# Linear-attention state added by one product of 384 columns instead of two of 192, with the step order laid out anew

## The chip, the cores and the metric

The kernel runs on one core of one Trainium2 chip. The metric is the device time of one execution in microseconds (us). It is launched several times; medians are given with the number of runs. The profile is one separate execution, so its span (start of the first to end of the last instruction) is not quite the time of a timed run. Where two kernels were timed in the same rounds on the same chip, the ratio is the mean of one kernel's fast runs over the mean of the other's fast runs of the same rounds. It is therefore not quite the ratio of the medians. A run counts as slow when it is over 1.5% above the fastest of its kernel.

TensorE is written PE in the profile, its weight loads PEld, VectorE DVE, ScalarE ACT, GpSimd POOL, SyncE SP. SP issues the loads.

## The reference

Two blocks follow one another. The first is a recurrent attention with a decay per step and channel, over 4 batches of 8 heads, 768 steps and 48 channels:

```
for t in range(S):
    cur = einsum('bhd,bhe->bhde', u * k[t], v[t])
    y[t] = einsum('bhd,bhde->bhe', r[t], state + cur)
    state = w[t][..., None] * state + einsum('bhd,bhe->bhde', k[t], v[t])
```

The second mixes the tokens of one batch (x is y with the heads side by side, 768 x 384):

```
W_tok = scale * (x @ w_q) @ (x @ w_k).T
out   = relu(W_tok @ x) @ w_out
```

## The kernel before

It works in 12 units of 256 steps, three per batch. A unit goes through some 30 steps on five engines: the log of w, running sums of it by matmul, exponentials, decayed r and k, transposes, the score matrix and its mask, the new state, the output. All matmuls go through one helper, so in the profile nearly all of TensorE has one line. Its groups are told apart by their tiles: cw are the running sums of the log (step `sums`), psT the transposes of decayed k and r (KdS, RdS), A the scores and AmB the masked ones, Sn the new state and SB the carried one, Y the output (`ymat` from the masked scores, `yst` from SB, `yd` from Vd), xt_ps, qk, Tps, mps and fps the products of the second block (fps is `fin`). A shape such as 64\*128 is the part of the array that a product uses, rows by columns. The parts that matter here:

```python
def load(n, nm, ap):                       # w, k, r, v of unit n, 384 KB each, from SyncE
    ...
    t = ld.tile([C, H, D2], F32, name=nm + "G", tag=nm + "G")     # 3 buffers each
    nc.sync.dma_start(out=t, in_=src.rearrange("h (p j) d -> p h (j d)", j=2))

def kdec(n):                               # GpSimd: decayed k, "Kd"
    nc.gpsimd.tensor_tensor(pad(T["Kd", n]), jhd(T["k", n]), hd(T["em", n]), ALU.mult)

def stadd(n, q):                           # adds the carried state to the new one, in PSUM
    if 2 * m + q:
        SB = T["SB", b, 2 * m + q]
        for hh in range(2):                # two products, each on 64 columns of the array
            mm(T["Sn", n][ds(hh * 64, 64), q, 0:DM].rearrange(...)[:, :, hh],
               ID128[:, ds(hh * 64, 64)],
               SB.rearrange(...)[:, :, hh], start=False)

def yst(n):                                # output from the state: full array
    ... mm(T["Y", n][:, q, ...], T["RKT", n][:, 0, q, hp], SB[:, ...], start=False)

def yd(n):                                 # output from u*k*r*v: 64 rows at a time
    ... mm(T["Y", n][:, q, 0:DM], PERM[ds(q * HC, HC), j], T["Vd", n][ds(q * HC, HC), j]...)
```

The order on every engine is fixed by a table. Each step has a time in the table (the unit's start plus an offset), all steps are sorted by it, and every engine executes its instructions in that order. The loads have a table of their own; only its order counts, together with the three buffers of each input:

```python
    steps = [ (-3.67, log, ()), (-1.33, uk1, ()), (-0.45, sums, ()), ...
              (15.25, ymat, ()), (15.48, yst, ()), (15.48, yd, ()), ... ]
    start  = [0.42, 8.84, 16.14, 23.73, 31.34, 38.86, ...]
    lstart = [-100, -99, -98, -11.4, -9.09, 4.54, 0.63, 6.68, 49.1, 51.23, 17.9, 58.9]
    ...
    for _, _, fn in sorted(plan, key=lambda x: x[:2]):
        fn()
```

## Time and profile before

| | kernel before |
|---|---|
| time, median of 3 runs | 123.15 us (122.78 to 123.25) |
| profiled span | 122.0 us, mean granted clock 0.971 |

Three lines of the page of the kernel before carry what the prediction only tells. The first is the busy time of each engine, its share of the span and its instructions. The second is the clock that TensorE was granted, in tenths of full speed, for 40 equal slices of the span. The third is the chain that ended last, by engine.
```profile
PE 100.1 (82%) x1822; PEld 64.6 (53%) x1822; DVE 91.8 (75%) x150; ACT 77.2 (63%) x146; POOL 84.7 (69%) x81
...
PEclk9999996799999999999999999999999999999985
...
PE 68%; ACT 12%; DVE 6%; DMA 3%; POOL 3%; issue 2%; ACTq 1%; SPq 1%; DVEq 0%
```
TensorE sets the pace of the middle of the kernel. By the page its clock falls once before the last slices, in the two slices from 18 to 24 us. The first products were slow too, though the page shows no lower clock there: two of 384 columns stood 0.33 us apart at 12.96 us, against 0.17 at 42.91.

### The profile page before, as it was taken

What the parts mean: (1) busy time and instruction counts of PE and PEld (TensorE: products, weight loads), DVE (VectorE), ACT (ScalarE), POOL (GpSimd) and SP (SyncE); (2) the same over time, 40 slices, a digit from 0 to 9 for tenths busy, and PEclk for the clock granted to TensorE, in tenths of its full rate; (3) what the DMA queues carried; (4) which work ended last, traced back from release to release, by engine and by line L of the source; (5) the groups of instructions that cost most, each with busy time, mean ns of one, the idle gap of its engine ahead of it and who ended that gap; (6) DMA issues with size and microseconds to landing.
All of it is one profiled execution on the core that took longest, in us unless ns stands there. A gap on an engine that the chain in (4) does not pass through costs nothing.

```text
span 122.0 us, 4284 instructions
## 1 busy us (share of the span) xinstructions
PE 100.1 (82%) x1822; PEld 64.6 (53%) x1822; DVE 91.8 (75%) x150; ACT 77.2 (63%) x146; POOL 84.7 (69%) x81
## 2 busy tenths in 40 slices
PE   0193938979898999999999899999999999966800
PEld 0133536557575766757657466576576666532400
DVE  6213596699798978999989998989989777253800
ACT  4236391689779868986685948976478966426000
POOL 8949899995999999599597995967839804000000
PEclk9999996799999999999999999999999999999985
DMA  3999999999999999899839999500552200573092
GB/s 77 322 325 325 323 320 341 292 232 318 236 256 273 288 300 263 230 266 247 245 75 329 348 269 252 149 0 0 134 129 52 82 5 0 129 181 85 24 283 83
DMA packets 54598, 24.66 MB, mean 202 GB/s; under 512 B 51121, under 2 KB 54578, under 8 KB 54578
## 3 DMA queue, kind: packets, MB, share of 16 engines
q1 hardware_dynamic: 52274, 21.24, 64.6%
q10 hardware_dynamic: 2304, 3.15, 9.1%
q8 instruction: 14, 0.23, 0.7%
q14 instruction: 6, 0.05, 0.1%
HBM read 19.66 MB, written 4.72 MB: 200 GB/s over the span
## 4 chain that ended last, share of the span: by engine, by line
PE 68%; ACT 12%; DVE 6%; DMA 3%; POOL 3%; issue 2%; ACTq 1%; SPq 1%; DVEq 0%
PE cw L66 12%; PE Y L66 11%; PE psT L66 10%; PE fps L66 10%; PE Sn L66 5%; PE A L66 5%; PE xt_ps L66 5%; PE qk L66 5%; PE Tps L66 4%; ACT X L130 3%; DMA u<-in_u_dram 3%; DVE AmB L244 3%; ACT XT L130 2%; PE mps L66 2%; POOL uk L250 1%
## 5 line engine op out<-in xcount | busy, mean ns | idle before, releaser
L244 DVE TENSOR_TENSOR AmB<-A,MASK 128x1024 bf16<-128x1024 f32 x24 | 28.8, 1219 | 1.3 <-PE A L66 1.2
L271 POOL TENSOR_TENSOR Vd<-V,diag 128x768 bf16<-128x768 bf16 x12 | 17.7, 1478 | 13.7 <-ACT X L130 3.4
L250 POOL TENSOR_TENSOR uk<-kG,ubc 128x768 f32<-128x768 f32 x12 | 21.8, 1816 | 1.7 <-DVE ubc L486 1.7
L178 ACT ACTIVATE em<-cw,bias 128x384 bf16<-128x384 f32 x24 | 13.0, 580 | 15.6 <-PE cw L66 15.6
L257 POOL TENSOR_TENSOR uk<-uk,rG 128x768 f32<-128x768 f32 x12 | 21.8, 1816 | 0.1
L207 POOL TENSOR_TENSOR KdS<-kG,em 128x768 bf16<-128x768 f32 x12 | 19.7, 1640 | 1.2 <-ACT em L178 1.2
L227 DVE COPY RKT<-psT 128x2048 bf16<-128x2048 bf16 x12 | 14.6, 1217 | 4.0 <-PE psT L66 4.0
L66 PEld LDWEIGHTS <-KdS 64*128 64x128 bf16 (+1 forms) x256 | 10.8, 99 | 9.1 <-POOL KdS L207 3.6
L200 DVE TENSOR_TENSOR RdS<-rG,cw 128x384 bf16<-128x384 f32 x24 | 12.2, 551 | 4.5 <-ACT cw L185 4.5
L66 PE MATMUL fps<-wout_sb,mixT 128*128 128x384 bf16 x72 | 14.6, 328 | 0.1
L302 DVE TENSOR_TENSOR SB<-Sn,pt 128x384 bf16<-128x384 f32 x20 | 11.0, 551 | 4.0 <-PE Sn L66 2.6
L66 PEld LDWEIGHTS <-RKT 48*64 48x64 bf16 (+1 forms) x464 | 10.3, 107 | 7.1 <-issue 4.5
L185 ACT ACTIVATE cw<-cw,bias 128x384 f32<-128x384 f32 x24 | 12.3, 553 | 0.2
L264 DVE TENSOR_REDUCE diag<-uk 128x16 f32<-128x768 f32 x12 | 11.3, 945 | 0.4 <-POOL uk L257 0.4
L155 ACT ACTIVATE logw<-wG 128x768 bf16<-128x768 f32 x12 | 10.2, 851 | 2.1 <-DMA wG<-in_w_dram 2.1
L66 PE MATMUL cw<-logw,BI 128*128 128x384 bf16 x36 | 11.5, 377 | 0.0
L66 PE MATMUL psT<-ID,KdS 128*128 128x128 bf16 x96 | 7.8, 227 | 4.0 <-DVE AmB L244 2.0
L66 PE MATMUL cw<-logw,BS 128*128 128x384 bf16 x36 | 11.0, 363 | 0.0
L66 PE MATMUL A<-RKT 48*64 48x128 bf16 x384 | 10.1, 226 | 0.8 <-ACT X L130 0.8
L130 ACT CAST X<-Y 128x768 bf16<-128x768 f32 x11 | 8.8, 800 | 2.9 <-PE Y L66 2.7
L211 ACT CAST V<-vG 128x768 bf16<-128x768 f32 x12 | 10.0, 841 | 0.0
L130 ACT COPY osb<-fps 128x384 f32<-128x384 f32 x13 | 6.1, 484 | 5.3 <-PE fps L66 2.1
(74 smaller groups left out, 165.1 us busy)
## 6 DMA issues: line engine op xcount, KB each, us to landing
wG<-in_w_dram SPq DMA_DIRECT2D x12, 384.0 KB, 5.5
kG<-in_k_dram SPq DMA_DIRECT2D x12, 384.0 KB, 5.1
rG<-in_r_dram SPq DMA_DIRECT2D x12, 384.0 KB, 4.8
vG<-in_v_dram SPq DMA_DIRECT2D x12, 384.0 KB, 4.9
out_dram<-osb ACTq DMA_DIRECT2D x16, 192.0 KB, 3.0
out_dram<-osb SPq DMA_DIRECT2D x8, 192.0 KB, 3.8
wout_f<-in_moe_w_out_dram SPq DMA_DIRECT2D x1, 576.0 KB, 4.7
wq_f<-in_moe_w_q_dram SPq DMA_DIRECT2D x1, 96.0 KB, 4.1
```

Source lines behind the costliest of these rows:

```text
L66: nc.tensor.matmul(o, l, rr, start=start, stop=stop, skip_group_check=True, is_transpose=trans)
L130: (nc.scalar.copy if e else nc.vector.tensor_copy)(o, i)
L178: nc.scalar.activation(em[:, j], T["cw", n, 1 + j][:, 0:DM], ACT.Exp, bias=bias[2 + j], scale=-1.0)
L185: nc.scalar.activation(cw, cw, ACT.Exp, bias=bias[j], scale=1.0)
L200: nc.vector.tensor_tensor(pad(Rd)[:, j], jhd(T["r", n])[:, j], T["cw", n, j][:, 0:DM].rearrange("p (h d) -> p h d", d=D), ALU.mult)
L207: nc.gpsimd.tensor_tensor(pad(T["Kd", n]), jhd(T["k", n]), hd(T["em", n]), ALU.mult)
L227: nc.vector.tensor_copy(RKT, T["psT", n])
L244: nc.vector.tensor_tensor(T["AmB", n][:, js].rearrange("p q h t -> p h q t"), T["A", n, js], _rep(_rep(MASK[:, js], 1, NP), 1, 2), ALU.mult)
L250: nc.gpsimd.tensor_tensor(uk, T["k", n].rearrange("p h (j d) -> p h j d", j=2), _rep(ubc.rearrange("p (h d) -> p h d", d=D), 2, 2), ALU.mult)
L257: nc.gpsimd.tensor_tensor(uk, uk, T["r", n].rearrange("p h (j d) -> p h j d", j=2), ALU.mult)
L264: nc.vector.tensor_reduce(diag.rearrange("p j h -> p h j"), T["uk", n], axis=AX.X, op=ALU.add)
L271: nc.gpsimd.tensor_tensor(Vd, T["V2", n], _rep(T["diag", n], 3, D), ALU.mult)
```

## The change

The intent: the two half-array products of `stadd` become one product over the whole array, which has the same shape as its usual neighbours, and the whole table of times is laid out anew around it.

```diff
-            for hh in range(2):
-                mm(T["Sn", n][ds(hh * 64, 64), q, 0:DM].rearrange(
-                    "p (q h d) -> p q h d", h=2, d=D)[:, :, hh],
-                   ID128[:, ds(hh * 64, 64)],
-                   SB.rearrange("p (q h d) -> p q h d", h=2, d=D)[:, :, hh], start=False)
+            mm(T["Sn", n][:, q, 0:DM], ID128, SB, start=False)
```

The new tables, cut to the rows that the argument uses:

```diff
     steps = [
-        (-3.67, log, ()),
-        (-1.33, uk1, ()),
-        (-0.45, sums, ()),
+        (-4.17, log, ()),
+        (-2.11, uk1, ()),
+        (-1.82, uk2, ()),
+        (-1.25, sums, ()),
         ...
-        (3.56, uk2, ()),
         ...
-        (15.25, ymat, ()),
-        (15.48, yst, ()),
-        (15.48, yd, ()),
+        (14.85, ymat, ()),
+        (14.88, yd, ()),
+        (15.08, yst, ()),
...
-    start = [0.42, 8.84, 16.14, 23.73, 31.34, 38.86, ...]
+    start = [0.58, 8.99, 16.15, 23.89, 31.49, 39.01, ...]
-    lstart = [-100, -99, -98, -11.4, -9.09, 4.54, 0.63, 6.68, 49.1, 51.23, 17.9, 58.9]
+    lstart = [-100, -99, -98, -17.38, -15.07, -5.06, -7.06, -6.47, 43.12, 46.19, 13.3, 52.91]
```

Cut away: the other rows of `steps`, the tables of the first and last unit and of the second block, four small tables that say whether ScalarE or VectorE makes a copy and which queue stores an output, the places of the weights' load and cast, a new layout of XT with the same element counts, and a transpose by DMA that stays switched off.

More of the change, by code (lines that the diff above doesn't have):

```diff
@@ L45 @@
     EX = (1, 1, 1, 1, 1, 1, 1, 1, 1, 1, 1, 0)
-    ET = (1, 1, 1, 1, 0, 0, 0, 0, 0, 1, 1, 0)
+    ET = (0, 1, 1, 1, 0, 0, 0, 0, 1, 1, 1, 0)
     EQ = (1, 0, 1, 0, 0, 0, 1, 0, 1, 1, 1, 0)
-    EM = (1, 1, 1, 0, 1, 0, 0, 1, 1, 0, 1, 1, 1, 1, 1, 1, 1, 1, 1, 0, 1, 1, 0, 1)
-    EF = (0, 1, 0, 1, 1, 1, 1, 0, 0, 1, 1, 0, 1, 1, 1, 1, 1, 1, 0, 0, 0, 0, 0, 0)
-    ES = (1, 0, 0, 1, 0, 1, 1, 1, 1, 1, 1, 0, 1, 1, 1, 1, 1, 1, 0, 1, 0, 1, 0, 0)
+    EM = (1, 1, 1, 0, 1, 0, 1, 0, 1, 0, 1, 1, 1, 1, 0, 1, 1, 1, 1, 0, 1, 1, 0, 1)
+    EF = (0, 1, 0, 1, 1, 1, 1, 0, 0, 1, 1, 0, 1, 1, 1, 1, 1, 1, 1, 1, 0, 0, 0, 0)
+    DT = (0, 0, 0, 0, 0, 0, 0, 0, 0, 0, 0, 0)
+    ES = (1, 0, 0, 1, 0, 1, 0, 1, 1, 1, 1, 0, 1, 1, 1, 0, 1, 0, 0, 1, 0, 1, 0, 0)
     NCH = S // C
@@ L343, in yev @@
             T["X", b] = xpool.tile([C, NCH, DM], BF16, name="X", tag="X")
-            T["XT", b] = xpool.tile([128, NK, S], BF16, name="XT", tag="XT")
+            T["XT", b] = xpool.tile([128, NCH, NK, C], BF16, name="XT", tag="XT")
             T["qk", b] = xpool.tile([128, NU, 4, DH], BF16, name="qks", tag="qks")
@@ L350, in xtr @@
         b, m = divmod(n, NU)
-        tp = mtile([128, NK, C2], BF16, "xt_ps")
+        if DT[n]:
+            nc.sync.dma_start_transpose(
+                out=T["XT", b][:, ds(2 * m, 2)].rearrange("p c k t -> p (c k) t"),
+                in_=T["X", b][:, ds(2 * m, 2)].rearrange("p c d -> p (c d)"))
+            return
+        tp = mtile([128, 2, NK, C], BF16, "xt_ps")
         for cc in range(2):
             for dt in range(NK):
-                mm(tp[:, dt, ds(cc * C, C)],
+                mm(tp[:, cc, dt],
                    T["X", b][:, 2 * m + cc, ds(dt * 128, 128)], ID128, trans=True)
@@ L360, in xev @@
         b, m = divmod(n, NU)
-        copy(ET[n], T["XT", b][:, :, ds(m * C2, C2)], T["tp", n])
+        if not DT[n]:
+            copy(ET[n], T["XT", b][:, ds(2 * m, 2)], T["tp", n])
     def qkmat(n):
@@ L371, in qkmat @@
             for kt in range(NK):
-                mm(qk[:, cc], XT[:, kt, ds((2 * m + cc) * C, C)], wk_sb[:, kt],
+                mm(qk[:, cc], XT[:, 2 * m + cc, kt], wk_sb[:, kt],
                    start=(cc == 0 and kt == 0))
@@ L376, in qkmat @@
                 mm(qk[ds(q * DH, DH), 2:4].rearrange("p c h -> p (c h)"), T["wq"][:, kt],
-                   XT[:, kt, ds((2 * m + q) * C, C)], start=False)
+                   XT[:, 2 * m + q, kt], start=False)
         T["qkp", n] = qk
@@ L501 @@
     steps = [
-        (-3.67, log, ()),
-        (-1.33, uk1, ()),
-        (-0.45, sums, ()),
-        (-0.42, expk, ()),
-        (-0.25, expr, ()),
-        (1.36, kdec, ()),
-        (1.89, rdec, ()),
-        (2.24, decay, ()),
-        (3.56, uk2, ()),
-        (5.7, trR, (1, )),
-        (5.95, trR, (0, )),
-        (5.99, vcast, ()),
-        (6.48, red, ()),
-        (6.51, vd, ()),
-        (7.46, evT, ()),
-        (8.59, amat, (0, )),
-        (9.91, amat, (1, )),
-        (10.1, mask, (0, )),
@@ L520 @@
-        (10.73, mask, (1, )),
-        (11.87, state, ()),
-        (11.9, stadd, (0, )),
-        (12.36, stev, (0, )),
-        (13.55, stadd, (1, )),
-        (14.38, stev, (1, )),
-        (15.25, ymat, ()),
-        (15.48, yst, ()),
-        (15.48, yd, ()),
-        (15.51, yev, ()),
-        (17.44, xtr, ()),
-        (18.18, xev, ()),
-        (20.45, qkmat, ()),
-        (20.75, qkev, ()),
+        (-4.17, log, ()),
+        (-2.11, uk1, ()),
+        (-1.82, uk2, ()),
+        (-1.25, sums, ()),
@@ new lines @@
+        (-0.85, expk, ()),
+        (-0.85, expr, ()),
+        (1.26, rdec, ()),
+        (1.84, decay, ()),
+        (2.32, kdec, ()),
+        (4.44, red, ()),
+        (5.37, trR, (1, )),
+        (5.66, trR, (0, )),
+        (6.06, vcast, ()),
+        (6.09, vd, ()),
+        (7.05, evT, ()),
+        (8.19, amat, (0, )),
+        (9.36, mask, (0, )),
+        (9.6, amat, (1, )),
+        (10.86, mask, (1, )),
+        (11.18, state, ()),
+        (11.21, stadd, (0, )),
+        (11.65, stev, (0, )),
@@ L534 @@
+        (13.15, stadd, (1, )),
+        (14.23, stev, (1, )),
+        (14.85, ymat, ()),
+        (14.88, yd, ()),
+        (15.08, yst, ()),
+        (15.11, yev, ()),
+        (16.78, xtr, ()),
+        (17.5, xev, ()),
+        (20.15, qkmat, ()),
+        (20.18, qkev, ()),
     ]
     first = [
-        (-6.23, log, ()),
-        (-6.05, sums, ()),
-        (-2.68, expk, ()),
-        (-0.31, decay, ()),
-        (0.59, uk1, ()),
-        (1.7, expr, ()),
-        (3.15, kdec, ()),
-        (5.93, trR, (1, )),
@@ L544 @@
-        (6.95, rdec, ()),
-        (6.98, trR, (0, )),
-        (7.64, evT, ()),
-        (8.73, uk2, ()),
-        (9.1, red, ()),
-        (9.65, amat, (0, )),
-        (9.93, amat, (1, )),
-        (11.0, mask, (0, )),
-        (12.22, mask, (1, )),
-        (13.97, vcast, ()),
-        (14.21, state, ()),
-        (14.64, stadd, (0, )),
-        (15.85, ymat, ()),
-        (16.28, stev, (0, )),
-        (16.31, stadd, (1, )),
-        (16.31, yst, ()),
-        (16.86, stev, (1, )),
-        (16.87, vd, ()),
@@ L562 @@
-        (16.9, yd, ()),
-        (17.07, yev, ()),
-        (18.09, xtr, ()),
-        (18.76, xev, ()),
-        (20.43, qkmat, ()),
-        (20.46, qkev, ()),
+        (-6.35, log, ()),
+        (-6.32, sums, ()),
+        (-6.09, uk1, ()),
+        (-3.08, expk, ()),
+        (-0.77, decay, ()),
+        (-0.04, expr, ()),
+        (2.81, kdec, ()),
+        (2.84, trR, (1, )),
+        (6.35, rdec, ()),
+        (6.57, trR, (0, )),
+        (7.24, evT, ()),
+        (8.41, uk2, ()),
+        (8.44, amat, (1, )),
@@ new lines @@
+        (9.38, amat, (0, )),
+        (10.72, vcast, ()),
+        (11.02, mask, (0, )),
+        (11.08, mask, (1, )),
+        (12.62, state, ()),
+        (14.92, stadd, (0, )),
+        (14.99, ymat, ()),
+        (15.05, red, ()),
+        (15.51, stev, (0, )),
+        (15.91, stadd, (1, )),
+        (15.91, yst, ()),
+        (15.94, stev, (1, )),
+        (16.43, vd, ()),
+        (16.46, yd, ()),
+        (16.49, yev, ()),
+        (17.69, xtr, ()),
+        (17.98, xev, ()),
+        (20.52, qkmat, ()),
@@ L568 @@
+        (20.69, qkev, ()),
     ]
     last = [
-        (-8.43, log, ()),
-        (-0.36, sums, ()),
-        (-0.33, expk, ()),
-        (0.3, expr, ()),
-        (0.33, rdec, ()),
-        (0.47, decay, ()),
-        (1.66, kdec, ()),
-        (5.38, vcast, ()),
-        (6.06, uk1, ()),
-        (6.69, trR, (0, )),
-        (7.03, trR, (1, )),
-        (7.36, evT, ()),
-        (7.73, uk2, ()),
-        (9.43, amat, (0, )),
-        (10.04, amat, (1, )),
-        (11.58, state, ()),
-        (13.51, red, ()),
@@ L587 @@
-        (14.13, mask, (0, )),
-        (15.69, stadd, (0, )),
-        (15.84, vd, ()),
-        (15.86, mask, (1, )),
-        (16.87, stev, (0, )),
-        (17.84, ymat, ()),
-        (17.87, yst, ()),
-        (17.87, yd, ()),
-        (21.51, stadd, (1, )),
-        (29.8, yev, ()),
-        (29.83, xtr, ()),
-        (33.23, xev, ()),
-        (33.26, qkmat, ()),
-        (33.29, qkev, ()),
-        (35.83, stev, (1, )),
+        (-10.35, log, ()),
+        (-0.76, sums, ()),
+        (-0.67, expk, ()),
@@ new lines @@
+        (-0.1, expr, ()),
+        (-0.03, rdec, ()),
+        (0.07, decay, ()),
+        (3.0, kdec, ()),
+        (3.24, uk1, ()),
+        (4.88, uk2, ()),
+        (5.38, trR, (0, )),
+        (6.14, trR, (1, )),
+        (7.3, vcast, ()),
+        (8.95, evT, ()),
+        (8.98, amat, (0, )),
+        (10.49, amat, (1, )),
+        (11.2, state, ()),
+        (11.46, red, ()),
+        (13.46, mask, (0, )),
+        (14.56, stadd, (0, )),
+        (15.48, vd, ()),
+        (15.48, mask, (1, )),
@@ L602 @@
+        (15.66, stev, (0, )),
+        (16.61, ymat, ()),
+        (17.49, yst, ()),
+        (17.51, yd, ()),
+        (21.0, stadd, (1, )),
+        (33.11, yev, ()),
+        (33.14, xtr, ()),
+        (33.58, xev, ()),
+        (33.61, qkmat, ()),
+        (36.61, stev, (1, )),
+        (38.07, qkev, ()),
     ]
@@ L605 @@
         (-0.17, tmat, (1, )),
-        (0.03, tmat, (2, )),
-        (0.67, tev, ()),
-        (1.72, mix, (0, )),
+        (-0.14, tmat, (2, )),
+        (0.85, tev, ()),
+        (1.13, mix, (0, )),
         (1.75, mixev, (0, 0, )),
-        (1.75, mixev, (0, 1, )),
-        (3.02, mix, (1, )),
+        (2.66, mix, (1, )),
+        (2.76, mixev, (0, 1, )),
         (3.05, mixev, (1, 0, )),
@@ L614 @@
         (5.18, mix, (2, )),
-        (5.5, mixev, (2, 0, )),
+        (5.21, mixev, (2, 0, )),
         (6.82, mixev, (2, 1, )),
-        (7.09, fin, (0, )),
-        (8.59, fin, (1, )),
-        (8.71, fin, (2, )),
+        (7.53, fin, (2, )),
+        (7.65, fin, (0, )),
         (9.55, finev, (0, )),
-        (9.58, finev, (1, )),
-        (12.6, finev, (2, )),
+        (9.96, fin, (1, )),
+        (9.99, finev, (1, )),
+        (11.75, finev, (2, )),
         (13.11, store, (0, )),
-        (13.4, fin, (3, )),
+        (13.34, fin, (3, )),
         (13.43, finev, (3, )),
-        (15.19, store, (1, )),
         (15.4, fin, (4, )),
-        (16.51, fin, (5, )),
-        (16.54, finev, (4, )),
+        (15.67, store, (1, )),
+        (15.9, finev, (4, )),
+        (17.07, fin, (5, )),
         (19.42, finev, (5, )),
@@ L633 @@
     blast = [
-        (12.66, tmat, (0, )),
-        (12.96, tmat, (1, )),
-        (13.44, tmat, (2, )),
-        (13.55, tev, ()),
-        (13.58, mix, (0, )),
-        (14.09, mix, (1, )),
-        (14.09, mix, (2, )),
-        (14.12, mixev, (0, 0, )),
-        (14.12, mixev, (0, 1, )),
-        (14.12, mixev, (1, 0, )),
-        (14.12, mixev, (2, 0, )),
-        (14.63, mixev, (1, 1, )),
-        (28.34, mixev, (2, 1, )),
-        (28.37, fin, (0, )),
-        (28.5, fin, (1, )),
-        (29.14, fin, (2, )),
-        (29.18, fin, (3, )),
-        (29.23, finev, (0, )),
-        (29.26, finev, (1, )),
-        (29.73, store, (0, )),
-        (29.74, fin, (4, )),
-        (30.7, finev, (2, )),
-        (31.09, finev, (3, )),
-        (31.34, fin, (5, )),
-        (33.84, store, (1, )),
-        (34.01, finev, (4, )),
-        (35.33, finev, (5, )),
-        (35.36, store, (2, )),
-    ]
-    start = [0.42, 8.84, 16.14, 23.73, 31.34, 38.86, 46.52, 54.11, 61.53, 69.25, 76.58, 84.42]
-    bstart = [40.55, 65.17, 85.94, 114.26]
-    lstart = [-100, -99, -98, -11.4, -9.09, 4.54, 0.63, 6.68, 49.1, 51.23, 17.9, 58.9]
+        (11.0, tmat, (0, )),
+        (11.3, tmat, (1, )),
+        (11.78, tmat, (2, )),
+        (11.9, tev, ()),
+        (11.93, mix, (0, )),
+        (11.96, mixev, (0, 0, )),
+        (11.96, mixev, (0, 1, )),
+        (12.43, mix, (1, )),
+        (12.43, mix, (2, )),
+        (12.46, mixev, (1, 0, )),
+        (12.46, mixev, (2, 0, )),
+        (12.98, mixev, (1, 1, )),
+        (26.69, mixev, (2, 1, )),
+        (26.72, fin, (0, )),
+        (26.85, fin, (1, )),
+        (27.35, finev, (0, )),
+        (27.48, fin, (2, )),
+        (27.6, finev, (1, )),
+        (27.69, fin, (3, )),
+        (28.07, store, (0, )),
+        (28.08, fin, (4, )),
+        (29.04, finev, (2, )),
+        (29.13, fin, (5, )),
+        (29.43, finev, (3, )),
+        (32.11, finev, (4, )),
+        (32.19, store, (1, )),
+        (33.67, finev, (5, )),
+        (33.7, store, (2, )),
+    ]
+    start = [0.58, 8.99, 16.15, 23.89, 31.49, 39.01, 46.67, 54.26, 61.68, 69.4, 77.03, 84.58]
+    bstart = [40.18, 64.95, 85.64, 114.04]
+    lstart = [-100, -99, -98, -17.38, -15.07, -5.06, -7.06, -6.47, 43.12, 46.19, 13.3, 52.91]
     for n in range(NT):
@@ L677 @@
     at(-99.0, ucast)
-    at(-67.84, wload)
-    at(19.23, wcast)
+    at(-69.89, wload)
+    at(18.55, wcast)
     with tc.manual_schedule():
```

## The prediction

> **What bounds the kernel now.** I read the stretches of the span first, then the chain that ended last, then single engines in order of time.
>
> The busy time in five stretches from 30 to 105 us (columns: PE, PEld, DVE, ACT, POOL busy, clock, DMA share, GB/s):
> ```profile
> 30.00:45.00 15.00, 13.47 (x320) 9.53 (x316) 13.29 (x17) 11.99 (x22) 14.96 (x10) 1.00 1.03 271
> 45.00:60.00 15.00, 15.00 (x272) 9.83 (x270) 14.30 (x22) 11.94 (x24) 12.12 (x8) 1.00 0.95 246
> 60.00:75.00 15.00, 14.45 (x296) 9.39 (x295) 13.72 (x20) 10.81 (x21) 13.18 (x9) 1.00 0.93 267
> 75.00:90.00 15.00, 14.72 (x295) 9.95 (x292) 14.47 (x21) 11.12 (x23) 10.88 (x7) 1.00 0.37 97
> ```
> TensorE (PE) has no spare time from 45 us on and VectorE is 0.3 to 1.3 us per 15 behind it. The DMA share is about 1 until 75 us: the 12 units' loads stream without a pause, and the first half of the kernel lives on what they deliver. The chain of waits agrees: PE holds 68% of it, ACT 12%, DMA only 3% (the very first load). From 45 to 68 us it is PE alone, so there every microsecond added to or taken from TensorE's program order counts, until VectorE becomes the bound.
>
> Now the piece that the title names, in TensorE's order of time:
> ```profile
> 57.41 0.62 PE L66 MATMUL psT<-ID,KdS 128*128 128x128 bf16 x8
> 57.87 0.61 PE L66 MATMUL psT<-ID,RdS 128*128 128x128 bf16 x8
> ...
> 65.44 0.61 PE L66 MATMUL psT<-ID,RdS 128*128 128x128 bf16 x8
> 65.98 0.27 PE L66 MATMUL Sn<-SB,ID 128*64 128x192 bf16 x2
> 66.18 0.34 PE L66 MATMUL cw<-logw,BI 128*128 128x384 bf16 x1
> ```
> Eight transposes take 0.46 us from start to start when a product of the same array shape (128\*128) follows, but 0.54 when the 128\*64 halves follow; the halves then hold the array for 0.20, though two of them lie on top of each other (270 ns each, 0.27 together).
>
> Last, the loads. SyncE issues, then ScalarE's logs of w, then TensorE where the log of unit 5 is used:
> ```profile
> 33.60 1.37 SPq L150 DMA_DIRECT2D wG<-in_w_dram  x1
> ...
> 39.34 1.14 SPq L150 DMA_DIRECT2D wG<-in_w_dram  x1
> 40.58 1.06 SPq L150 DMA_DIRECT2D kG<-in_k_dram  x1
> ```
> ```profile
> 40.77 0.85 ACT L155 ACTIVATE logw<-wG 128x768 bf16<-128x768 f32 x1
> ```
> ```profile
> 42.45 0.62 PE L66 MATMUL psT<-ID,RdS 128*128 128x128 bf16 x8
> 42.91 0.33 PE L66 MATMUL cw<-logw,BI 128*128 128x384 bf16 x1
> ```
> ```profile
> wG<-in_w_dram SPq DMA_DIRECT2D x12, 384.0 KB, 5.5
> ```
> Counting from the start, 33.60 is the seventh issue of w and 39.34 the eighth. Sorting the kernel's load table gives the order of units 0, 1, 2, 3, 4, 6, 5, 7, 10, 8, 9, 11: the seventh is unit 5, the eighth unit 7. The log at 40.77 is the sixth, so unit 5's. Its w landed at about 33.60 + 5.5 = 39.1 (the trace's completion event: 39.37), 1.4 us before use.
>
> **What the Trainium skill says.** "TensorEngine Tiling (Array Packing)", section Key Properties: "Changing tiling mode (not just tile) drains the TensorE". The trace agrees; the drains are the 0.08 and 0.12 us worked out below. The same page's Restrictions say that column tiling disables the fast weight load; here the 64-column load of the identity took 106 ns, the 128-column one 98, so next to nothing hangs on it. "DMA: Bandwidth & Descriptors", section Queues, rings and completion order: on each DMA engine descriptors are consumed in ring order. The completion events agree: SyncE's loads land in the order of issue, 1.2 to 2.5 us apart, so a load's place in the queue fixes its time. "TensorE: Matmul & The Clock Gate", Part 1: the clock falls to half after an idle window of about 3.4 us. The trace has one such case: PE idle for 2.02 us up to 18.17 and again 0.53 before 19.30, then products of 384 columns 0.31 to 0.32 us apart instead of 0.165 until about 22.6.
>
> **The change part by part.**
>
> Product over 128 columns. There are 16 state additions (four per batch). Each was two products of 192 columns side by side. Estimate of their array time: half of the 0.165 us that separates two 384-column products, 0.08. One product of 384 columns: 0.165. So 16 x 0.08 = 1.3 us are added. What goes is changes of array shape. A change costs 0.54 - 0.46 = 0.08 going in, 0.20 - 0.08 = 0.12 coming out; from six fps to the state's products it is 1.08 - 6 x 0.165 = 0.09. I take 0.10. I sorted both step tables into TensorE's order and counted where the shape changes: 159 before, 129 after. Of the 30, 20 belong to the one product, whose shape is that of transposes, sums and fins. 20 x 0.10 - 1.3 = 0.7 us saved. The off-diagonal blocks that it now adds as well are zeros (the decay's -100 terms), so the result stays right.
>
> Step order. Ten of the 30 changes go because the Vd product now stands next to ymat, which has its shape, ahead of the state product: 1.0 us saved. TensorE altogether: 1.7 us, of which about 1.3 after 43 us.
>
> GpSimd: the second uk multiply now follows the first directly (81 us in all, unchanged), so the row sum is ready a step sooner and Vd too. The waits before Vd (13.7 us) were not on the chain: worth nothing. At the start it pushes Vd of units 1 and 0 back by one multiply (1.8 us), to about 24.5, where the Vd product of unit 0 started at 23.93; TensorE, which now makes both transposes of unit 1 after the state product at half clock, gets there at about the same time. Estimate for the start: 0 to +0.5 us.
>
> Evacuations: XT of unit 0 moves to VectorE and of unit 8 to ScalarE (800 against 550 ns), one relu moves to VectorE, two output copies at the end to ScalarE, three stores from ACT's queue to SyncE's. At the tail TensorE paces the fins at 0.49 and VectorE copies at 0.48, so two copies less free nothing. The new XT layout keeps element counts and types. Sum: -0.1 us.
>
> The load table. Here is what I think decides. The new keys give 0, 1, 2, 3, 4, 6, 7, 5, 10, 8, 9, 11: unit 5 goes behind unit 7, the log of unit 5 does not move in ScalarE's order, and the sums of unit 5 do not move in TensorE's (after the transposes of unit 4, ahead of ymat of unit 3). The eighth w lands at 39.34 + 5.5 = 44.8 (event: 44.99), its k at 46.1, its r at about 47.3. Nothing ahead of it in the queue shrinks and the DMA share is about 1, so I see nothing to bring it forward. The log then runs 45.0 to 45.9, and TensorE starts the sums at 45.9 in place of 42.91: +3.0 us, with both engines in order and nothing to pull ahead. GpSimd follows: uk of unit 5 from 46.1 (before: 41.42), second multiply, Vd of 4, then Kd of 5: 46.1 + 1.8 + 1.8 + 1.45 + 1.6 = 52.7. TensorE wanted it at 49.30, now at 49.30 + 3.0 - 0.2 = 52.1: +0.6 us. After that GpSimd has caught up with TensorE's new time.
>
> Sum: +3.0 + 0.6 for the late load; -1.3 from TensorE after 43 us, of which VectorE (95% busy from 45 to 90) lets through perhaps 0.8. What is saved before 43 us only lengthens the wait for the load. Net +2.8, so about 125.9.
>
> **The rivals.**
> 1. The saving arrives and the load is harmless: DMA runs faster than before, or the queue has room. For it: 384 KB every 1.2 us in the first 17 us, against 1.2 to 2.5 later; at that rate throughout, the eighth w would land near 40. Against: it did not run so in this trace, though SyncE issued without idling. Then -0.8 to -1.5: 121.6 to 122.4.
> 2. VectorE becomes the bound and eats the saving, load harmless: 122.5 to 123.2.
> 3. The wait also drops the clock: 3.5 us of idle TensorE (42.4 to 45.9) is over one window, as at 16 to 19 us. Half clock for 3.4 us costs up to 1.7 us, less what lies under the wait for Kd: 126.5 to 127.5.
>
> **Range and chances.** The late load follows from queue order and in-order engines, so I give it three in four; the rest is for a faster queue, and for a retuned order that was perhaps chosen because it ran well. With the load late, I expect 124.8 to 127.5, the upper part if the clock drops (even odds); without, 121.6 to 123.2. Predicted 125.8 us, range 122.0 to 127.6. Faster than 120.7: 0.04, even all of TensorE's saving does not reach it. Slower than 125.6: 0.56. Within 2%: 0.40.
>
> **What would show it.** Right on the load: a wait of ScalarE for the DMA of w, 3 to 4 us long, near 41 to 45 us; GpSimd idle near 40 to 46; a gap in PE of about 3 us ahead of the sums. Wrong: the sixth log at 41 us or earlier. Right on the product: Sn<-SB as 128\*128, 128x384, x16, about 0.16 us to the next start, eight transposes ahead of it 0.46. Right on the order: ymat to the Vd product without the extra 0.1. Clock: a slice under full speed near 46 to 50 us. If VectorE is the limit, its idle time from 50 us on falls while PE shows new gaps. I am wrong altogether if the span is shorter by over 1.7 us, which would mean a latency that I took as hidden was not.

## The result, and the profile after

| | before | after |
|---|---|---|
| time, median of 4 runs each, same rounds | 122.97 us (122.71 to 123.25) | 127.21 us (126.81 to 128.01) |
| ratio of fast runs, 95% interval | 1 | 1.0353 (1.0294 to 1.0412) |
| profiled span | 122.0 us | 125.2 us, clock 0.96 |

The changed kernel is 3.5% slower. The result is correct.

The same three lines of the page, and then the two windows that differ most (columns as in the prediction), of the changed kernel:
```profile
PE 99.8 (80%) x1806; PEld 64.2 (51%) x1806; DVE 90.9 (73%) x149; ACT 78.3 (62%) x147; POOL 85.1 (68%) x81
...
PEclk9999996899999995999999999999999999999995
...
PE 60%; DMA 8%; POOL 8%; ACT 8%; DVE 8%; issue 3%; SPq 1%; DVEq 0%; ACTq 0%
```
```profile
30.00:45.00 15.00, 12.12 (x277) 8.60 (x276) 13.42 (x18) 8.95 (x16) 9.59 (x6) 1.00 1.01 266
45.00:60.00 15.00, 12.99 (x238) 7.95 (x238) 9.37 (x15) 12.40 (x24) 12.50 (x8) 0.89 0.67 179
```
No engine has much more to do: the busy times are those of before within 1.2 us. The chain has lost PE and gained DMA (3 to 8%), and the clock has a second dip, in the sixteenth slice (47 to 50 us). From 45 to 60 us TensorE is busy for 13.0 us instead of 15.0, VectorE for 9.4 instead of 14.3, and the DMA share falls from 0.95 to 0.67. So work waited there, and the loads with it: each input has three buffers, and a load can't start before one of them is free.

The trace names the wait. SyncE's eighth issue of w, ScalarE's log of unit 5, GpSimd's first multiply with k of unit 5, and TensorE's sums of unit 5 (columns: start, time, engine, line, operation, tiles, shape, count, idle time before and what ended it):
```profile
39.66 1.11 SPq L152 DMA_DIRECT2D wG<-in_w_dram  x1
```
```profile
46.12 0.84 ACT L157 ACTIVATE logw<-wG 128x768 bf16<-128x768 f32 x1 [4.58 <-DMA wG<-in_w_dram]
```
```profile
47.34 1.81 POOL L252 TENSOR_TENSOR uk<-kG,ubc 128x768 f32<-128x768 f32 x1 [7.32 <-DMA kG<-in_k_dram]
...
52.43 1.64 POOL L209 TENSOR_TENSOR KdS<-kG,em 128x768 bf16<-128x768 f32 x1
```
```profile
42.38 0.61 PE L68 MATMUL psT<-ID,KdS 128*128 128x128 bf16 x8
42.85 0.32 PE L68 MATMUL Sn<-SB,ID 128*128 128x384 bf16 x1
43.01 0.61 PE L68 MATMUL psT<-ID,RdS 128*128 128x128 bf16 x8
47.01 0.48 PE L68 MATMUL cw<-logw,BI 128*128 128x384 bf16 x1 [3.39 <-ACT logw L157]
47.28 0.52 PE L68 MATMUL cw<-logw,BS 128*128 128x384 bf16 x1
...
54.72 0.62 PE L68 MATMUL psT<-ID,KdS 128*128 128x128 bf16 x8
```
Unit 5's w is issued at 39.66 and landed at 46.09 (39.37 before). The log waits 4.58 us for it, and TensorE 3.39 us for the log. After that wait the 384-column products start 0.27 and 0.32 us apart; before the change the same two stood 0.17 apart. The clock had dropped. The lines at 42 us show the new product itself: eight transposes now hold the array for 0.47 us and the product for 0.16, where the halves took 0.54 and 0.20.

Five points of the profiled executions, in us, show what carried through ("sums" and "transposes" are the starts of TensorE's sums and first transposes of unit 5, "k ready" the end of GpSimd's Kd of unit 5, "end" the end of the last output copy on VectorE):

| | sums | k ready | transposes | sums to transposes | end |
|---|---|---|---|---|---|
| before | 42.91 | 46.27 | 49.30 | 6.39 | 116.21 |
| after | 47.01 | 54.07 | 54.72 | 7.71 | 120.18 |

### The profile page after: what moved, and what is told of

Same layout as the page of the kernel before. It is cut to its first block, busy times and chain, and to the rows that moved or that the text cites. A ratio compares the mean times of both kernels' runs of the same rounds, so it can differ in the third digit from the quotient of the medians.

```text
span 125.2 us, 4240 instructions
## 1 busy us (share of the span) xinstructions
PE 99.8 (80%) x1806; PEld 64.2 (51%) x1806; DVE 90.9 (73%) x149; ACT 78.3 (62%) x147; POOL 85.1 (68%) x81
## 4 chain that ended last, share of the span: by engine, by line
PE 60%; DMA 8%; POOL 8%; ACT 8%; DVE 8%; issue 3%; SPq 1%; DVEq 0%; ACTq 0%
PE cw L68 10%; PE Y L68 10%; PE fps L68 9%; PE psT L68 8%; DMA wG<-in_w_dram 5%; PE A L68 4%; PE Sn L68 4%; PE qk L68 4%; PE xt_ps L68 4%; PE Tps L68 3%; POOL uk L252 3%; DVE AmB L246 3%; DMA u<-in_u_dram 3%; POOL KdS L209 3%; ACT cw L187 2%
## 5 line engine op out<-in xcount | busy, mean ns | idle before, releaser
L68 PE MATMUL cw<-logw,BS 128*128 128x384 bf16 x36 | 11.8, 386 | 0.0
L132 ACT COPY osb<-fps 128x384 f32<-128x384 f32 x15 | 7.1, 483 | 3.6 <-PE fps L68 1.9
```

The source lines that it names most:

```text
L68: nc.tensor.matmul(o, l, rr, start=start, stop=stop, skip_group_check=True, is_transpose=trans)
L132: (nc.scalar.copy if e else nc.vector.tensor_copy)(o, i)
```

## The experiments

The theory: the late load of unit 5 is the whole loss. It costs the wait for w and the slow clock behind it; without it the change would be a small gain. The rivals: the new step order, above all of the first units, is itself slower; or GpSimd, held up by k, is the cause and TensorE's wait only the part that shows. All runs gave correct results. The kernel before was run beside each call: 123.43 us on the first chip (11 runs), 123.39 on the second, 123.55 on the third, the last one noisier (123.18 to 125.83).

### First call: the load, the clock and the product, one at a time

**e1_unit5_ahead**: the changed kernel with the loads of units 5 and 7 changing places.

```diff
-    lstart = [..., -17.38, -15.07, -5.06, -7.06, -6.47, 43.12, ...]
+    lstart = [..., -17.38, -15.07, -6.47, -7.06, -5.06, 43.12, ...]
```

> The changed kernel, with the loads of unit 5 put ahead of those of unit 7 again and nothing else touched. Late load as the cause: the log of unit 5 starts at about 41.5 us with no wait for its DMA, the gap of PE ahead of the sums of unit 5 goes, and so does the low clock after it; about 122.5 us, 121.8 to 123.3. Rival, the new step order is bad by itself and the wait for the load only shows where it is: 125 us or more, with a gap of like size elsewhere.

Measured: 122.30 us (6 runs, 122.10 to 123.24), ratio 0.9917 (0.9872 to 0.9963). ScalarE and TensorE in its trace:
```profile
41.28 0.85 ACT L157 ACTIVATE logw<-wG 128x768 bf16<-128x768 f32 x1
```
```profile
43.30 0.33 PE L68 MATMUL cw<-logw,BI 128*128 128x384 bf16 x1
```
Neither line has a bracket: no idle time before them. Two numbers of the load table changed, and 4.9 us went by the medians (127.21 - 122.30), 5.4 by the ratios (4.4% of 123). The load's place is the whole slowdown, and without it the change is 0.8% faster than before (0.4 to 1.3% by the interval).

The table of points gives the same sum. This kernel has sums at 43.30, transposes at 49.65 (6.35 later) and its end at 115.20. Against it the changed kernel loses 3.71 us up to the sums (47.01 - 43.30), 1.36 us more up to the transposes (7.71 - 6.35), together 5.07, and 4.98 at the end. So nothing of the loss was regained afterwards, and nothing further was lost.

**e2_before_unit5_late**: the opposite, the kernel before with the same two loads changing places.

```diff
-    lstart = [..., 4.54, 0.63, 6.68, ...]     # units 5, 6, 7
+    lstart = [..., 6.68, 0.63, 4.54, ...]
```

> The kernel before, with the loads of unit 5 put behind those of unit 7 and nothing else touched. Late load as the cause: ScalarE waits about 4 us for w at the log of unit 5, PE stands about 3 us before its sums; 126 to 128 us. Rival, the old step order has the slack to take a late load: under 125 us.

Measured: 129.60, 125.60, 129.47 and 127.20 us; of the two fast ones the ratio is 1.0237 (1.0154 to 1.0319). The profiled run is one of the slow ones. ScalarE and TensorE in it:
```profile
46.05 0.84 ACT L155 ACTIVATE logw<-wG 128x768 bf16<-128x768 f32 x1 [5.32 <-DMA wG<-in_w_dram]
```
```profile
46.95 0.48 PE L66 MATMUL cw<-logw,BI 128*128 128x384 bf16 x1 [4.00 <-ACT logw L155]
```
The same wait appears in the old kernel, with none of the other changes. Its size is not settled by this run: the four times spread over 4 us, the wait was profiled in a slow run only, and the two slow runs also had the lower mean clock (0.948 and 0.947, against 0.980 and 0.968).

**e3_late_but_warm**: the changed kernel, load late, with 18 extra products of 384 columns ahead of the sums of unit 5. They write to the bank that the sums overwrite, and keep TensorE busy during the wait.

```diff
             cw = T["cw", n, i] = mtile([C, 512], F32, f"cw{i}")
             od = cw[:, 0:DM].rearrange("p (h d) -> p h d", d=D)
+            if n == 5 and i == 1:
+                old = pad(LW[(n - 1) % NB])
+                for _ in range(18):
+                    mm(od, ID128, old[:, 0])
```

> The changed kernel with 18 products of 384 columns ahead of the sums of unit 5, into the PSUM that these then overwrite (start flag), so that TensorE isn't idle while it waits for the load; the result stays right. They take 18 x 0.165 = 3.0 us of a 3.4 us wait. If the half clock after the wait costs by itself: the sums and ymat after it run at full clock (384-column products 0.165 us apart, not 0.31), and the time falls by 1.0 to 1.7 us, to about 125.8. If the low clock lies under the wait for Kd of unit 5 and costs nothing: 127.0 to 127.4, unchanged.

Measured: 125.51 us (6 runs, 125.32 to 126.44), ratio 1.0186 (1.0141 to 1.0232): 1.7 us less than the changed kernel by the medians, 2.1 by the ratios. TensorE and, below, the log on ScalarE in its profile:
```profile
43.35 3.09 PE L68 MATMUL cw<-logw,ID 128*128 128x384 bf16 x18
46.28 0.33 PE L68 MATMUL cw<-logw,BI 128*128 128x384 bf16 x1
```
```profile
43.42 0.84 ACT L157 ACTIVATE logw<-wG 128x768 bf16<-128x768 f32 x1 [1.98 <-DMA wG<-in_w_dram]
```
The sums take 0.33 us, not 0.48, so the clock has stayed up, and from sums to transposes it is 6.35 us again (52.63 - 46.28). So the slow clock costs 1.36 us there. The gain is not the clock's alone, though. In this run w happened to land at 43.40 and its log was done at 44.26 (43.42 + 0.84); from then on it was the extra products, and no longer the load, that held the sums, until 46.28. So the profiled run is not quite a test of a warm TensorE with the load as late as before. The sums start 0.73 us sooner than in the changed kernel's run; 0.73 + 1.36 = 2.09 is the 2.07 by which its last copy ends sooner (118.11). Had only the clock stayed up in the changed kernel's run, TensorE would have reached the transposes at 47.01 + 6.35 = 53.36 and waited for k until 54.07. By this estimate the clock made no more than 0.65 us of that run's loss visible; the rest lay over the wait for k.

**e4_before_one_product**: the kernel before with the one product alone.

```diff
-            for hh in range(2):
-                mm(T["Sn", n][ds(hh * 64, 64), q, 0:DM]..., ID128[:, ds(hh * 64, 64)], ..., start=False)
+            mm(T["Sn", n][:, q, 0:DM], ID128, SB, start=False)
```

> The kernel before with the one product over 128 columns and nothing else changed. From the counts of shape changes: 0.7 us less TensorE work, of which 0.4 to 0.7 us arrives: 122.3 to 122.6. Rival, VectorE or the waits between engines take it: 122.8 to 123.1, no change. Other rival, a 128-column product has no drain to save: 1.3 us more TensorE work, 123.5 to 124.2.

Measured: 122.34 us (6 runs, 122.19 to 122.46), ratio 0.9907 (0.9872 to 0.9942), so 1.1 us saved, with an interval of 0.7 to 1.6. The piece of TensorE's order that the prediction showed from 65.44 us of the kernel before, here:
```profile
64.70 0.61 PE L66 MATMUL psT<-ID,RdS 128*128 128x128 bf16 x8
65.15 0.33 PE L66 MATMUL Sn<-SB,ID 128*128 128x384 bf16 x1
65.31 0.33 PE L66 MATMUL cw<-logw,BI 128*128 128x384 bf16 x1
```
From transposes to sums it is 0.61 us in place of 0.74: 0.13 saved. The product is worth what it promised, alone and without any new order. Added up place by place as in the next run, these two traces give about 0.6 us (17 shape changes fewer here, not 20); what the rest of the measured 1.1 is was not traced.

### Second call: the parts of the new order, with the load on time

**e5_e1_halves**: e1_unit5_ahead with the two halves put back (the diff of the product, reversed).

> The changed kernel with unit 5's loads ahead (122.3 us), and the state addition in two halves of 64 columns again. The product saves by the shape changes it removes, in the new order as in the old (where it saved 1.1 us): 123.0 to 123.5. Rival, the new order hides the drains: 122.3 to 122.6.

Measured: 123.29 us (6 runs, 123.27 to 123.99), ratio 0.9988 (0.9953 to 1.0024). Against 0.9917 that is 0.7% or 0.9 us for the product in the new order; the two intervals just touch, so the traces have to carry it. Of 16 places, 7 have full-array shapes on both sides and save 0.13 each. One goes from a full-array shape to 64 rows (0.04 saved), five from 64 rows to the full array (0.03 saved each), and at three the product stands between products of 64 rows and costs 0.07 more. 7 x 0.13 + 0.04 + 5 x 0.03 - 3 x 0.07 = 0.9. (The four places before 35 us, where waits or the slow clock differ between the two traces, are counted like the others of their kind.)

**e6_e1_yst_first**: e1_unit5_ahead with yst ahead of yd again, so that the shape changes once more per unit.

```diff
-        (14.88, yd, ()),
-        (15.08, yst, ()),
+        (14.88, yst, ()),
+        (15.08, yd, ()),
```

> The changed kernel with unit 5's loads ahead (122.3 us), and the state product put ahead of the Vd product again for units 1 to 10, so that ten shape changes come back. If each costs 0.1 us of TensorE's path: 122.9 to 123.3. Rival, VectorE has become the limit and the ten drains lie under its waits: 122.2 to 122.5.

Measured: 123.39 us (6 runs, 123.29 to 123.76), ratio 0.9989 (0.9953 to 1.0026): 0.9 us slower than e1_unit5_ahead by the ratios, 1.1 by the medians.

**e7_e4_yd_first**: the other way round, e4_before_one_product with yd ahead of yst.

```diff
         (15.25, ymat, ()),
-        (15.48, yst, ()),
         (15.48, yd, ()),
+        (15.48, yst, ()),
```

> The kernel before with the one product (122.34 us), and the Vd product put ahead of the state product for units 1 to 10, nothing else. Ten shape changes less: 121.4 to 121.9, if TensorE's path is what counts. Rival as in the run before: 122.2 to 122.5.

Measured: 121.32 us (6 runs, 121.22 to 122.03), ratio 0.9827 (0.9792 to 0.9863). TensorE's output step of one unit, first without and then with this swap:
```profile
59.50 0.57 PE L66 MATMUL Y<-V,AmB 64*128 64x48 bf16 x32
60.01 0.51 PE L66 MATMUL Y<-SB,RKT 128*128 128x96 bf16 x8
60.45 0.50 PE L66 MATMUL Y<-Vd,PERM 64*128 64x384 bf16 x4
60.88 0.42 PE L66 MATMUL A<-RKT 48*64 48x128 bf16 x16
```
```profile
59.49 0.57 PE L66 MATMUL Y<-V,AmB 64*128 64x48 bf16 x32
59.91 0.49 PE L66 MATMUL Y<-Vd,PERM 64*128 64x384 bf16 x4
60.33 0.51 PE L66 MATMUL Y<-SB,RKT 128*128 128x96 bf16 x8
60.77 0.42 PE L66 MATMUL A<-RKT 48*64 48x128 bf16 x16
```
The same three groups take 1.38 us in one order and 1.28 in the other. The group of 64x48 products gives up its place after 0.42 instead of 0.51 us when a group of the same shape (64\*128) follows. Ten units make 1.0 us, and 1.0 us (0.8% by the ratios) came out at the end. This version is the best and beats both kernels: 121.32 us against 123.39 of before on the same chip. It is two small edits away from the kernel before.

Against e1_unit5_ahead, which has the same two savings, it is 0.9% faster: the rest of the new order costs about 1.1 us. e6_e1_yst_first against e4_before_one_product, the same pair without the swap, says nearly the same (0.9989 against 0.9907, 1.0 us). The next run looks for it.

**e8_e1_uk2_later**: e1_unit5_ahead with GpSimd's second multiply of units 1 and 2 at its old place. In the new order it stands ahead of the Vd multiply of unit 0, for which TensorE waits in the trace of e1_unit5_ahead:
```profile
24.50 0.50 PE L68 MATMUL Y<-Vd,PERM 64*128 64x384 bf16 x4 [1.13 <-POOL Vd L273]
```
```diff
         for dt, fn, a in (first if n == 0 else last if n == NT - 1 else steps):
+            if fn is uk2 and n in (1, 2):
+                dt = 3.56
```

> The changed kernel with unit 5's loads ahead (122.3 us), and the second uk multiply of units 1 and 2 put back to where it stood before on GpSimd, so that Vd of unit 0 comes 1.8 us sooner. The trace shows PE waiting 1.13 us for that Vd at 24.5 us. If this wait is on the path: it goes, and the time falls by 0.7 to 1.1 us, to 121.2 to 121.6. Rival, ScalarE's weight casts and the masks behind it are as late anyway: 122.1 to 122.4.

Measured: 121.97 us (6 runs, 121.64 to 122.28), ratio 0.9870 (0.9836 to 0.9904). The wait is gone (the same product starts at 23.66, without a bracket), but only 0.3 us by the medians, 0.6 by the ratios, of the hoped for 0.7 to 1.1 came, and the intervals of the two runs overlap. A new wait for a mask took part of its place:
```profile
26.27 0.52 PE L68 MATMUL Sn<-V,KdS 64*128 64x96 bf16 x16 [0.35 <-DVE AmB L246]
...
27.86 0.61 PE L68 MATMUL psT<-ID,KdS 128*128 128x128 bf16 x8 [0.35 <-DVE AmB L246]
```
Before the edit the first of these lines stood at 26.68 without a bracket. So of 0.84 us at the Vd product (24.50 to 23.66) 0.41 is left two steps later. The second wait is not new: it stood at 28.27 in e1_unit5_ahead, and one of 0.27 for the state's copy follows in both.

### Third call: what lies beneath the wait for w, and three tries at a faster version

**e10_only_w_ahead**: the changed kernel with only w of unit 5 early; its k, r and v stay late.

```diff
-            at(lstart[n] + 0.01 * i, lambda n=n, nm=nm, ap=ap: load(n, nm, ap))
+            tl = -6.48 if (n, nm) == (5, "w") else lstart[n]
+            at(tl + 0.01 * i, lambda n=n, nm=nm, ap=ap: load(n, nm, ap))
```

> The changed kernel with only the w of unit 5 put ahead of unit 7's loads; its k, r and v stay late. ScalarE's wait at the log goes. If the late k is a second stall of its own, which the wait for w merely covers: GpSimd waits for k until about 47.3 us, Kd of unit 5 is done at about 54.0 where TensorE wants it at 49.65, and the kernel is as slow as the changed one, 126.5 to 127.7. If only w was on the path: 122.3 to 123.0.

Measured: 128.75 us (4 runs, 128.24 to 129.30), ratio 1.0414 (1.0361 to 1.0467): no gain at all, 0.6% more than the changed kernel on another chip. The sums of unit 5 start without a wait at 43.72. VectorE, then TensorE, after that:
```profile
49.01 1.02 DVE L202 TENSOR_TENSOR RdS<-rG,cw 128x384 bf16<-128x384 f32 x2 [3.50 <-DMA rG<-in_r_dram]
49.95 2.35 DVE L246 TENSOR_TENSOR AmB<-A,MASK 128x1024 bf16<-128x1024 f32 x2
```
```profile
51.22 0.69 PE L68 MATMUL Sn<-V,KdS 64*128 64x96 bf16 x16 [1.94 <-DVE AmB L246]
...
54.30 1.03 PE L68 MATMUL psT<-ID,KdS 128*128 128x128 bf16 x8 [0.63 <-DVE diag L266]
```
With w on time, r and k hold the kernel instead. VectorE waits 3.50 us for r of unit 5, and the masks of unit 4 stand behind that in its order; TensorE waits 1.94 us for them. Then it waits 0.63 us at the transposes. The bracket there names VectorE's row sum, which ended at 54.27; GpSimd's Kd of unit 5, which these transposes read, ended at 54.24. So Kd alone would have held TensorE about as long, and the trace can't tell the two apart. TensorE reaches the transposes at 54.30, only 0.42 us sooner than in the changed kernel, with a slow clock from 51.4 us on (the transposes take 1.03 us, not 0.61). The rival that GpSimd is the cause is half right: behind the wait for w there are two more for the same unit, on r and on k, that hold TensorE back nearly as far. The opposite, w late with k and r on time, was not run.

**e9_e7_loads_in_order**: e7_e4_yd_first, whose log of unit 5 starts only 0.11 us after its w has landed, with units 5, 6, 7 loaded in that order.

```diff
-    lstart = [..., 4.54, 0.63, 6.68, ...]
+    lstart = [..., 0.63, 4.54, 6.68, ...]
```

> The kernel before with the one product and the Vd product first (121.32 us), and the loads of units 5, 6, 7 in the order of their use. In the trace of 121.32 us unit 5's w landed at 40.24 and its log began at 40.35, so with no slack left; a unit's place sooner gives some 5 us. If that was costing: 121.0 to 121.3 and less spread; if not: 121.2 to 121.5. A later load of unit 6 (log at 48 us) does no harm.

Measured: 122.28 us (6 runs, 121.56 to 122.92), ratio 0.9901 (0.9852 to 0.9950). No gain is shown. The call was noisy, and its interval just overlaps that of e7_e4_yd_first; whether the order of these loads matters while all are in time stays open.

**e11_e8_xt0_on_act**: e8_e1_uk2_later with the XT copy of unit 0 on ScalarE, as before the change (`ET[0]` 0 to 1), to see whether moving it to VectorE cost the rest of the start.

> The changed kernel with unit 5's loads ahead and the two uk multiplies later (121.97 us), and the XT copy of unit 0 on ScalarE again. It stands on VectorE between the two masks of unit 1, and PE then waits 0.35 us for a mask and 0.27 for the state at 28 to 29 us. If that is the rest of what the start lost: 121.3 to 121.6. Rival, ScalarE with its weight casts is as late with 0.8 us more: 121.9 to 122.3.

Measured: 121.68 us (6 runs, 121.49 to 122.34), ratio 0.9851 (0.9811 to 0.9891), against 0.9870: no clear gain. TensorE's wait moved to the copy's new place:
```profile
28.02 0.35 PE L68 MATMUL qk<-wk_sb,XT 128*128 128x64 bf16 x6 [0.55 <-ACT XT L132]
```
So no gain from this copy is shown. What remains of the start's cost, some 0.5 us (0.43%) between e8_e1_uk2_later and e7_e4_yd_first, was not traced to one step.

**e12_e9_u_first**: e9_e7_loads_in_order with u loaded first, from ScalarE's queue.

```diff
+    nc.scalar.dma_start(out=u1, in_=u.rearrange("h d -> (h d)"))
     nc.scalar.preload_act_table_set("natural_log_exp_and_others")
...
-    at(-99.985, uload)
```

> The run with loads in order (about 121.2 us), and the load of u issued first, from ScalarE's queue, in place of third on SyncE's. The first piece of the chain of waits is 3.55 us for this DMA of 1.5 KB, which sits behind two of 384 KB. If it lands 2 us sooner, ubc, uk and Kd of unit 0 come sooner and everything after: 119.5 to 120.5. Rival, the k load (5.3 us) and the exponentials (9.4) hold Kd of unit 0 as long: 121.0 to 121.3.

Measured: 121.94 us (6 runs, 120.94 to 122.91), ratio 0.9837 (0.9783 to 0.9892), 0.6% below e9_e7_loads_in_order with wide overlap; the 119.5 to 120.5 hoped for did not come. In its trace u landed at 2.29 instead of some 5.2 us, and the first transposes stood at 9.59 instead of 10.94. By the output products of unit 0 all of it was gone (22.05 against 21.85), because TensorE then waited 3.15 us for masks in place of 2.39 and ran slow for longer. This profile is of a run of 122.39 us with a mean clock of 0.964. Two of the six runs took 120.94 and 120.95 us, with 0.976 and 0.974. So what the edit is worth when the clock falls for a shorter time stays open.

## Why the prediction was right or wrong

Slower was right, and so was the time: 127.21 us is inside 122.0 to 127.6 and 1.4 above 125.8. Being inside says little by itself, because that range held both outcomes of the load; what the prediction risked was the 0.56 for slower than 125.6. The mechanism at its centre is shown by e1_unit5_ahead, which takes it away, and by e2_before_unit5_late, which puts it into the old kernel. Step by step:

- **Late load, +3.0 us**: right in place and kind, too small. The log waited for the DMA of w (4.58 us), TensorE for the log (3.39), GpSimd for k (7.32), about where it was written. But w landed at 46.09, not 45.0: a load's place in the queue, which the prediction took to fix its time, fixed only its order here. The sums started 4.1 us later than before, 3.7 later than with the load on time.
- **Clock (rival 3)**: it happened, and the even odds left it out of the central figure. From sums to transposes of unit 5 it took 1.36 us more (7.71 against 6.35), inside the "up to 1.7 us, less what lies under the wait for Kd". This and the later landing are the term that the sum was short of. By the estimate at e3_late_but_warm the two causes overlap: at full clock Kd of unit 5 would have kept 0.7 of the 1.4 us.
- **Wait for Kd, +0.6**: not seen in the changed kernel, where Kd was ready 0.65 us before TensorE came, because the slow clock had held TensorE up. With w alone on time (e10_only_w_ahead) a wait of 0.63 us stood there, for Kd and the row sum together, and before it one through VectorE for r that the prediction did not have.
- **One product, -0.7**: 0.9 by e5_e1_halves in the order that the step had counted, 1.1 by e4_before_one_product in the old one. The count of 20 shape changes was right (149 against 129 in the two traces of the new order); a place between two full-array neighbours saved 0.13, not 0.12, and the extra array time at the others was charged a little too high.
- **yd next to ymat, -1.0**: 0.9 to 1.1 by e6_e1_yst_first, 1.0 by e7_e4_yd_first, 0.10 us for each unit in the trace.
- **VectorE lets 0.8 of 1.3 through**: wrong. The two savings together brought 2.1 us in e7_e4_yd_first (1.73% of 123.4), against 1.7 predicted for TensorE. VectorE, busy for 14.8 of 15 us from 45 to 60 there, took nothing back. The reading behind this step was off as well: by the lines that the prediction shows, VectorE's busy time is 0.3 to 0.7 us below TensorE's, and 1.3 is VectorE's own idle time from 60 to 75 us.
- **Start, 0 to +0.5**: too small. The new order without its two good parts costs about 1.1 us, of which GpSimd's order of multiplies may explain 0.3 to 0.6 (e8_e1_uk2_later, not clear of the noise).
- **Three readings of its traces** were loose. The landings of the loads stand 1.1 us apart at the closest (44.99 and 46.10), not 1.2. Four of the five stretches that it announces are shown. And the clock's fall at 19 us was no case of an idle window: TensorE was busy for 0.92 of the 3.41 us before it.
- **Rivals 1 and 2** (the load harmless) fell. Their times, 121.6 to 123.2, are what the change gives when the load is on time: 122.30.

So the sum came so close partly by luck, because terms that were off cancelled. Against the kernel before it should have read: +3.7 for the load, +1.4 for the clock, -2.1 for TensorE, +1.1 for the start, together +4.1; the medians differ by 4.2.

## What to carry to other kernels

A table of times is also an order: when a schedule is laid out anew, sort the loads by their new keys and compare which unit each place in the queue belongs to, for a swap of two of them here cost about 5 us and turned a gain of 1 into a loss of 4. Before putting a wait down to one late transfer, ask what else of the same unit is late: with w alone brought forward, r and k held the same point within 0.4 us. And a wait of TensorE can cost more than its length, because the products after it may run at a lower clock; read the distance between two known points after the wait, here 7.7 us against 6.4.

## What the Trainium skill lacked or had wrong

- "TensorEngine Tiling (Array Packing)", Key Properties, says that a change of tiling mode drains TensorE, but not what a drain costs. Here one change cost about 0.1 us: 0.13 saved at a place that loses two changes and gains about 0.08 of array time, and 0.10 for each unit whose output step has one change less.
- "TensorE: Matmul & The Clock Gate", Part 1, gives one idle window of about 3.4 us for the fall to half clock. The wait of 3.39 us in the changed kernel fits it, but the window need not be idle. In the kernel before, TensorE was busy for 0.92 us of the 3.41 before the clock fell (15.83 to 19.24 us), in e10_only_w_ahead for 1.20 (48.00 to 51.41), in e5_e1_halves for 2.04 (23.28 to 26.69). How busy is busy enough, these runs don't settle.
- None of the pages looked up tells how far the landing of one load varies between runs. The eighth w of twelve, at the same place of the queue, landed between 43.4 and 46.8 us in the traces of twelve kernels that have nearly the same program up to then. They are single executions and not all on one chip, so how much of this is due to the program, the chip or chance stays open. A transfer that is only just in time in one profile is therefore not known to be in time.
